# Fourier mixing with a gated feed-forward block: the output product as seven half-size products for eight, with its sums on GpSimd and its result transposed on VectorE

## The chip, the cores and the metric

The kernel runs on one core of one Trainium2 chip. The metric is the device time of one execution in microseconds. A core has TensorE (matmuls, and weight loads beside them), VectorE (called DVE in the profile), ScalarE (ACT), GpSimd (POOL) and SyncE (SP), which issues DMAs. SBUF is the working memory, PSUM the memory in banks that matmuls write to.

## What is computed

The reference, cut to what matters:

```python
batch, seq, dim = (8, 3008, 256)               # x, float32
X = np.fft.fft(np.fft.fft(x, axis=1), axis=2).real.astype(np.float32)
x = X.reshape(24064, 256)
gate = 1.0 / (1.0 + np.exp(-(x @ w_gate)))     # w_gate, w_val: 256 x 1536
val = x @ w_val
return (gate * val @ w_out).astype(np.float32) # w_out: 1536 x 256
```

All matmuls are float32.

## The kernel before, in words

**Prologue.** The sequence transform uses that the real part of the result is even in the sequence position: for each of the 8 batches only positions 0 to 1504 (`NK` = 1505) are computed, and each gives two output rows, `k` and its mirror `S - k`. `fold_x` (L180) adds and subtracts mirrored sequence positions and features of the input in place in the tile `x4`, and writes the feature-folded halves to the tiles `wp` and `wq`. For batch 0 it runs on VectorE. `half` (L208) then does one matmul group of the sequence transform with the table `st`: six matmuls into two PSUM banks `ev` and `od`, a copy of `ev` to `a` by ScalarE, and two VectorE instructions (L216, L219) that write the sum and the difference to every second column of the tiles `pk` and `qk`; a third tile, `ek`, holds feature 128. The weights arrive as 64-bit floats; `weight_ops` (L109) turns each piece into float32 with work on VectorE and GpSimd, and `merge` (L141) multiplies the gate and value weights with the feature transform once, into `G1`, `G2` and `ge`. The last six of the eighteen pieces are `w_out`, which goes to the tile `wo`.

**Main loop.** The positions of a batch are cut into six chunks, five of 256 and one of 225, and the 1536 hidden features into 12 tiles of 128. A step is one (batch, chunk, feature tile): 576 steps, numbered by the loop at L352. `front` (L259) does four matmuls into two banks `pa` and `pb` (for gate and value), two `scalar_tensor_tensor` instructions that make `ae` from `pa` (L272), two VectorE instructions that make `z` from `ae` and `pb` (L275 the position, L276 its mirror), and the sigmoid of the gate half of `z` on ScalarE (L277). `gate` (L280) multiplies the gate by the value to give `h` (L283); it is issued one step later, ahead of the next step's `front`. `back` (L286) multiplies `h` with `wo` into `po`, with `h` as the stationary operand and `wo` as the moving one, so that tokens are the rows of the result: four matmuls of 128 rows by 256 columns for a step, three steps after its `front` (`LAG`, L349). The trace counts two instructions for each float32 matmul. After the twelfth feature tile `store` (L298) copies `po` to SBUF on ScalarE and issues the output DMAs on SP.

Each engine takes its instructions in the order in which the code issues them. The four banks of `psx` go round among `pa`, `pb`, `ev` and `od`; the four of `pso` hold `po` of two chunks, two banks each.

**Side work.** The dictionary `side` (L334) places work for the next batch at steps: `fold_x` of the next batch on GpSimd after step 1 of a batch (one list of large instructions, L185 to L198), the load of the batch after that at step 12, and the groups of the sequence transform (`seq_ops`, L222) spread over the later steps. In the first batch `e_fold` and `e_rows` add the rows that `ek` needs for the other seven.

Of the kernel before, what the change touches and what calls it, by code (L numbers as in the profile page):

```python
# [13 lines left out]
PSUM = bass.MemoryType.PSUM  # L14

# [19 lines left out]
def kernel(  # L35
# [19 lines left out]
    NFT = F // P  # L55
    CH = 256
    WC = 256
    HD = D // 2
    assert D == 256 and M % 4 == 0 and NP * NQ > M // 2 and NQ % 2 == 0
# [7 lines left out]
    fold = ctx.enter_context(tc.tile_pool(name="fold", bufs=1))  # L67
# [5 lines left out]
    hp = ctx.enter_context(tc.tile_pool(name="hp", bufs=4))  # L73
    osp = ctx.enter_context(tc.tile_pool(name="osp", bufs=4))
    psx = ctx.enter_context(tc.tile_pool(name="psx", bufs=4, space=PSUM))
    pso = ctx.enter_context(tc.tile_pool(name="pso", bufs=4, space=PSUM))
# [17 lines left out]
    wo = const.tile([P, NFT, D], F32, name="wo")  # L94
# [5 lines left out]
    er = const.tile([B - 1, NK], F32, name="er")  # L100
# [8 lines left out]
    def weight_ops(src, out):  # L109
# [6 lines left out]
        exp = osp.tile([P, 2, WC], F32, name="exp", tag="os")  # L116
# [38 lines left out]

    def load_weights():
        jobs = []
        for c in range(F // WC):
            for g, w in enumerate((moe_w_gate, moe_w_val)):
                jobs.append((w[:, c * WC : (c + 1) * WC], g, c))  # L160
        for c in range(NFT // 2):
            jobs.append((moe_w_out[2 * c * P : 2 * (c + 1) * P, :], None, c))
        rest = []
        for src, g, c in jobs:
            if g is None:
                ws = wo[:, 2 * c : 2 * c + 2, :]
            else:
                ws = app.tile([P, 2, WC], F32, name="ws", tag="ae")
            first, then = weight_ops(src, ws)
            first()  # L170
            for f in rest:
                f()
            rest = [then] + ([] if g is None else [lambda ws=ws, g=g, c=c: merge(ws, g, c)])
        for f in rest:
            f()
# [4 lines left out]
    def fold_x(b, eng):  # L180
        x4 = X.pop(b)
        tt = eng.tensor_tensor

        def point(i, j):
            tt(x4[:, i, :, 1:D], x4[:, i, :, 1:D], x4[:, j, :, D - 1 : 0 : -1], op=ALU.add)  # L185
            tt(x4[:, i, :, 0], x4[:, i, :, 0], x4[:, j, :, 0], op=ALU.add)

        point(0, 1)
        point(2, 3)
        tt(x4[:, 1], x4[:, 0], x4[:, 2], op=ALU.add)  # L190
        tt(x4[:, 3], x4[:, 0], x4[:, 2], op=ALU.subtract)
        for blk in range(2):
            v = x4[:, 1 + 2 * blk]
            wp = fold.tile([NP, NQ, HD], F32, name="wp", tag=f"wp{blk}")
            wq = fold.tile([NP, NQ, HD - 1], F32, name="wq", tag=f"wq{blk}")
            tt(wp[:, :, 1:HD], v[:, :, 1:HD], v[:, :, D - 1 : HD : -1], op=ALU.add)  # L196
            eng.tensor_copy(wp[:, :, 0], v[:, :, 0])
            tt(wq, v[:, :, 1:HD], v[:, :, D - 1 : HD : -1], op=ALU.subtract)  # L198
            W[b, blk] = (wp, wq)
            if b == 0:  # L200
                we = hp.tile([NP, NQ, P], F32, name="we", tag="we")
                eng.tensor_copy(we, v[:, :, HD : HD + 1].to_broadcast([NP, NQ, P]))  # L202
                W[b, blk] += (we,)
# [4 lines left out]
    def half(w, d, blk, sn, rows):  # L208
        c0, n = ((0, NE), (NE, NO))[blk]
        ev, od = bank("ev")[0:rows, 0:n], bank("od")[0:rows, 0:n]  # L210
        for o, par in ((ev, 0), (od, 1)):
            for q in range(par, NQ, 2):
                mm(o, w(q), st[:, int(sn), q, c0 : c0 + n], q == par, q >= NQ - 2)
        a = evp.tile([P, NE], F32, name="a", tag="a")[0:rows, 0:n]
        nc.scalar.copy(a, ev)
        nc.vector.tensor_tensor(d[:, blk : blk + 2 * n - 1 : 2], a, od, op=ALU.add)  # L216
        lo, hi = (od, a) if sn else (a, od)
        top = M - blk
        nc.vector.tensor_tensor(d[:, top : top - 2 * NO + 1 : -2], lo[:, 0:NO], hi[:, 0:NO],  # L219
                                op=ALU.subtract)  # L220

    def seq_ops(b):  # L222
        def start():
            PQE[b] = (pqp.tile([P, NK], F32, name="pk", tag="pk"),
                      pqp.tile([HD - 1, NK], F32, name="qk", tag="qk"),
                      pqp.tile([P, NK], F32, name="ek", tag="ek"))
            if b:
                nc.sync.dma_start(out=PQE[b][2], in_=ed[b - 1 : b, :].to_broadcast([P, NK]))

        def group(blk, what):  # L230
            rows = HD - 1 if what == 1 else P
            return lambda: half(lambda q: W[b, blk][what][:, q, :], PQE[b][what], blk, what == 1,
                                rows)

        return [start] + [group(blk, what) for blk in range(2) for what in range(2 if b else 3)]


# [11 lines left out]
    def e_rows(blk):  # L249
        half(lambda q: x8[:, :, 1 + 2 * blk, q], er, blk, False, B - 1)  # L250
        if blk:
            nc.scalar.dma_start(out=ed, in_=er)
# [3 lines left out]
    steps = [(b, c, f) for b in range(B) for c in range(len(chunks)) for f in range(NFT)]  # L256
    PO = {}

    def front(b, c, f):  # L259
        k0, n = chunks[c]  # L260
        ks = slice(k0, k0 + n)
        fs = slice(f * P, (f + 1) * P)
# [15 lines left out]
        return b, c, f, z  # L278

    def gate(b, c, f, z):  # L280
        n = chunks[c][1]
        h = hp.tile([P, 2, CH], F32, name="h", tag="h")[:, :, 0:n]
        nc.vector.tensor_tensor(h, z[:, 0], z[:, 1], op=ALU.mult)  # L283
        return b, c, f, h

    def back(b, c, f, h):  # L286
        n = chunks[c][1]
        if f == 0:
            PO[b, c] = [pso.tile([P, 2, D], F32, name="po", tag="po") for _ in range(2)]
        for s in range(2):  # L290
            for j, t0 in enumerate(range(0, n, P)):
                m = min(P, n - t0)
                mm(PO[b, c][s][0:m, j, :], h[:, s, t0 : t0 + m], wo[:, f, :],
                   f == 0 and j == 0, f == NFT - 1)
        if f == NFT - 1:
            store(b, c, PO.pop((b, c)))

    def store(b, c, po):  # L298
        k0, n = chunks[c]
        for s in range(2):  # L300
            os_ = osp.tile([P, 2, D], F32, name="os", tag="os")
            lo, hi, r0 = 0, n, b * S + k0
            if s:
                r0 = b * S + S - k0 - n + 1
                lo = 1 if k0 + n == NK else 0
                hi = n - 1 if k0 == 0 else n
            if n == 2 * P:
                nc.scalar.copy(os_, po[s])  # L308
            else:
                for j, t0 in enumerate(range(0, n, P)):  # L310
                    m = min(P, n - t0)
                    nc.scalar.copy(os_[0:m, j], po[s][0:m, j])
            if (lo, hi) == (0, 2 * P):
                nc.sync.dma_start(out=out[r0 : r0 + n, :].rearrange("(j p) d -> p j d", p=P),
                                  in_=os_)
                continue
            for j, t0 in enumerate(range(0, n, P)):
                p0, p1 = max(lo - t0, 0), min(hi - t0, P)
                pm = p0 + (p1 - p0) // 16 * 16
                for u0, u1 in ((p0, pm), (pm, p1)):  # L320
                    if u0 < u1:
                        nc.sync.dma_start(out=out[r0 + t0 + u0 : r0 + t0 + u1, :],
                                          in_=os_[u0:u1, j, :])


    fold_x(0, nc.vector)
    for f in seq_ops(0):
        f()
    load_weights()
# [3 lines left out]
    per = len(chunks) * NFT  # L333
    side = {}  # L334
    for b in range(B - 1):
        s0 = b * per
        side.setdefault(s0 + 1, []).append(lambda b=b: fold_x(b + 1, nc.gpsimd))
        if b + 2 < B:
            side.setdefault(s0 + NFT, []).append(lambda b=b: load_x(b + 2))
        f0 = 2 * NFT  # L340
        if b == 0:
            f0 = 3 * NFT + 6
            side.setdefault(f0 - 10, []).append(e_fold)
            for blk in range(2):
                side.setdefault(f0 - 6 + 2 * blk, []).append(lambda blk=blk: e_rows(blk))
        for i, f in enumerate(seq_ops(b + 1)):
            side.setdefault(s0 + f0 + i * (per - f0 - 4) // 5, []).append(f)

    LAG = 3  # L349
    fresh = None  # L350
    ready = []
    for i, step in enumerate(steps):  # L352
        if fresh is not None:
            ready.append(gate(*fresh))
        fresh = front(*step)
        if len(ready) >= LAG:
            back(*ready.pop(0))
        for f in side.get(i, []):
            f()
    ready.append(gate(*fresh))  # L360
    for r in ready:
        back(*r)
# [49 lines left out]
```

## Time and profile before

| what | value |
|---|---|
| median of three runs | 2286.54 us (2284.35 to 2288.05) |
| the profiled execution | 2285.57 us |
| its span, first to last instruction | 2283.8 us |
| mean granted clock of TensorE | 0.988 |
| ScalarE busy | 431.3 us, 19% |
| GpSimd busy | 236.9 us, 10% |
| the chain that ended last, by engine | PE 68%, DVE 23%, ACT 4%, DMA 2% |

The span is the time between the first and last instruction of the profiled execution; the 1.8 us between it and the time of that execution lie around it. "Busy" is the time in which an engine had an instruction running; matmuls are pipelined and their ends are modelled, so TensorE's busy time is not its time at its peak. "Idle" is the time just before an instruction in which its engine had nothing to do, and the releaser named behind the arrow is what the instruction waited for. In the groups, "128x512 f32<-128x512 f32" is the shape written and read, in partitions by elements, and L283 is line 283 of the kernel.

### The profile page before, as it was taken

The page shows a single profiled execution, that of the slowest core. Times are in us where ns is not written, and L with a number is a line of the kernel's source. Part 1 is how long each engine was busy: PE and PEld are TensorE (multiplying, and loading weights), DVE is VectorE, ACT ScalarE, POOL GpSimd, SP SyncE. Part 2 cuts the span into 40 slices and gives each one's busy share as a digit, 9 for nine tenths or more (in the row PEclk, how much of TensorE's full clock was granted, in tenths as well). Part 3 has the DMA queues.
Part 4 walks back from the last instruction along what each step waited for, and adds up shares of the span by engine and source line. Part 5 has one row for each costly group of instructions (what it writes and reads, how often), then busy time and mean ns, then how long its engine had stood idle before and what let it go on. Part 6 is the DMA issues. An engine that isn't in the chain of part 4 may idle for free.

```text
span 2283.8 us, 26007 instructions
## 1 busy us (share of the span) xinstructions
PE 2199.2 (96%) x9840; PEld 1840.4 (81%) x9840; DVE 1717.3 (75%) x3056; ACT 431.3 (19%) x762; POOL 236.9 (10%) x146
## 2 busy tenths in 40 slices
PE   4759999999999999999999999999999999999998
PEld 2648788888887888888888888878888888888887
DVE  3977777777777777777777777777777777777776
ACT  0111121112112111211211121112112111211211
POOL 0980001200002000020002000020000000000000
PEclk9779999999999999999999999999999999999999
DMA  5350010100001000110001000010000000000000
GB/s 166 117 132 10 10 33 10 63 23 19 10 10 63 32 10 10 39 57 10 10 19 63 23 19 10 10 63 33 10 10 18 23 10 10 19 9 10 19 10 18
DMA packets 56340, 70.86 MB, mean 31 GB/s; under 512 B 24117, under 2 KB 48437, under 8 KB 53948
## 3 DMA queue, kind: packets, MB, share of 16 engines
q1 hardware_dynamic: 34384, 64.26, 8.2%
q10 hardware_dynamic: 21832, 4.94, 1.1%
q8 instruction: 79, 1.29, 0.2%
q14 instruction: 45, 0.37, 0.1%
HBM read 44.50 MB, written 24.68 MB: 30 GB/s over the span
## 4 chain that ended last, share of the span: by engine, by line
PE 68%; DVE 23%; ACT 4%; DMA 2%; issue 1%; ACTq 1%; DVEq 0%
PE po L79 31%; PE pb L79 16%; PE pa L79 15%; DVE h L283 6%; DVE ae L272 6%; DVE z L275 5%; ACT z L277 4%; DVE z L276 4%; PE ev L79 3%; PE od L79 3%; DMA st<-in_stab_dram 1%; ACTq L240 1%; DVE man L130 1%; DVE man L133 0%; DVE man L132 0%
## 5 line engine op out<-in xcount | busy, mean ns | idle before, releaser
L79 PE MATMUL po<-wo,h 128*128 128x256 f32 (+1 forms) x4608 | 1091.0, 379 | 1.4 <-DVE h L283 1.3
L79 PEld LDWEIGHTS po<-wo,h 128*128 128x128 f32 (+1 forms) x4608 | 864.9, 188 | 127.3 <-DVE h L283 2.3
L283 DVE TENSOR_TENSOR h<-z 128x512 f32<-128x512 f32 (+1 forms) x576 | 423.3, 735 | 411.5 <-ACT z L277 411.5
L277 ACT ACTIVATE z<-z 128x512 f32<-128x512 f32 (+1 forms) x576 | 357.9, 621 | 1721.5 <-DVE z L276 1721.5
L79 PE MATMUL pa<-pk,G 128*128 128x256 f32 (+1 forms) x2304 | 585.2, 376 | 28.8 <-DVE ae L272 28.8
L79 PE MATMUL pb<-qk,G 127*128 127x256 f32 (+1 forms) x2304 | 601.0, 383 | 5.4 <-DVE z L276 5.2
L79 PEld LDWEIGHTS pa<-pk,G 128*128 128x128 f32 x2304 | 437.5, 190 | 96.3 <-DVE ae L272 32.6
L79 PEld LDWEIGHTS pb<-qk,G 127*128 127x128 f32 x2304 | 420.5, 190 | 111.5 <-issue 56.2
L272 DVE SCALAR_TENSOR_TENSOR ae<-ek,ge,pa 128x256 f32<-128x256 f32 (+1 forms) x1152 | 492.1, 468 | 0.0
L275 DVE TENSOR_TENSOR z<-ae,pb 128x512 f32<-128x512 f32 (+1 forms) x576 | 389.9, 677 | 61.0 <-DVE ae L272 1.4
L276 DVE TENSOR_TENSOR z<-ae,pb 128x512 f32<-128x512 f32 (+1 forms) x576 | 385.4, 669 | 0.0
L196 POOL TENSOR_TENSOR wp<-x 126x762 f32<-126x762 f32 x14 | 26.1, 1867 | 752.3 <-PE od L79 752.3
L185 POOL TENSOR_TENSOR x<-x 126x1530 f32<-126x1530 f32 x14 | 48.2, 3445 | 302.7 <-DMA x<-in_xf_dram 302.7
L198 POOL TENSOR_TENSOR wq<-x 126x762 f32<-126x762 f32 x14 | 25.3, 1807 | 364.3 <-PE od L79 364.3
L79 PE MATMUL ev<-st,wp 126*128 126x377 f32 (+1 forms) x96 | 35.1, 502 | 24.3 <-DMA st<-in_stab_dram 24.3
L79 PE MATMUL ps<-ws,dt 128*128 128x256 f32 (+1 forms) x96 | 31.8, 490 | 17.8 <-DVE ws L137 9.6
L79 PEld LDWEIGHTS ev<-st,wp 126*128 126x128 f32 x96 | 18.9, 198 | 34.1 <-DVE we L202 24.3
L308 ACT COPY os<-po 128x512 f32<-128x512 f32 x80 | 42.2, 578 | 0.0
L79 PEld LDWEIGHTS ps<-ws,dt 128*128 128x128 f32 (+1 forms) x96 | 22.0, 240 | 22.3 <-issue 18.2
L128 POOL TENSOR_SCALAR exp<-exp 128x512 int32<-128x512 f32 x18 | 36.6, 2031 | 1.5
L79 PE MATMUL ev<-st,wq 126*127 126x377 f32 (+1 forms) x96 | 33.1, 480 | 1.5 <-DMA st<-in_stab_dram 1.5
L79 PE MATMUL od<-st,wp 126*128 126x377 f32 (+1 forms) x96 | 33.6, 486 | 0.0
(58 smaller groups left out, 415.1 us busy)
## 6 DMA issues: line engine op xcount, KB each, us to landing
x<-in_xf_dram SPq DMA_DIRECT2D x16, 1512.0 KB
out_dram<-os SPq DMA_DIRECT2D x72, 256.0 KB
ek<-ed SPq DMA_DIRECT2D x7, 752.5 KB
st<-in_stab_dram ACTq DMA_DIRECT2D x2, 2223.7 KB
raw<-in_moe_w_gate_dram SPq DMA_DIRECT2D x6, 512.0 KB
raw<-in_moe_w_val_dram SPq DMA_DIRECT2D x6, 512.0 KB
raw<-in_moe_w_out_dram SPq DMA_DIRECT2D x6, 512.0 KB
out_dram<-os SPq DMA_DIRECT2D x16, 128.0 KB
```

The lines of the kernel that those rows point to most:

```text
L79: nc.tensor.matmul(o, l, r, start=start, stop=stop, skip_group_check=True)
L128: nc.gpsimd.tensor_scalar(out=expi, in0=exp, scalar1=0.0, scalar2=255.0 * 2.0 ** 23, op0=ALU.max, op1=ALU.min)
L130: ts(out=mani, in0=hi, scalar1=0xFFFFF, scalar2=3, op0=ALU.bitwise_and, op1=ALU.logical_shift_left)
L185: tt(x4[:, i, :, 1:D], x4[:, i, :, 1:D], x4[:, j, :, D - 1 : 0 : -1], op=ALU.add)
L196: tt(wp[:, :, 1:HD], v[:, :, 1:HD], v[:, :, D - 1 : HD : -1], op=ALU.add)
L198: tt(wq, v[:, :, 1:HD], v[:, :, D - 1 : HD : -1], op=ALU.subtract)
L272: nc.vector.scalar_tensor_tensor(out=ae[:, g], in0=ek[:, ks], scalar=ge[:, g, f : f + 1], in1=pa[:, g], op0=ALU.mult, op1=ALU.add)
L275: nc.vector.tensor_tensor(z[:, :, 0], ae, pb, op=ALU.add)
L276: nc.vector.tensor_tensor(z[:, :, 1, ::-1], ae, pb, op=ALU.subtract)
L277: nc.scalar.activation(z[:, 0], z[:, 0], AF.Sigmoid)
L283: nc.vector.tensor_tensor(h, z[:, 0], z[:, 1], op=ALU.mult)
L308: nc.scalar.copy(os_, po[s])
```

## The change

**The output product.** Two feature tiles make a pair (`NPR` = 6 pairs for a chunk). For a pair, the product of the two token halves (position and mirror), the two feature tiles and the two halves of the output columns is a 2 by 2 by 2 block product. It is now done with Strassen's seven block products (in the form with shared sums) for eight. Four sums of `h` are made on GpSimd in `gate` for each pair: one after the first `h` of the pair, three after the second, each of 128x256. Four sums of `w_out`'s blocks are made once, on GpSimd, in `forms`, which also copies three blocks on VectorE. The weights are now the stationary operand and the sums of `h` the moving one, so the result has output columns as rows and tokens as columns. Seven tiles accumulate over the six pairs of a chunk, in four PSUM banks `po0` to `po3`; there is one set of them.

**After a chunk**, `finish` copies the seven tiles to SBUF on ScalarE (four copies), and puts ten entries on the list `later`, one of which is issued at the end of each step: five GpSimd instructions that combine the seven products, then four VectorE transposes in 32x32 blocks, and the stores, now of 64 floats at a time. For the last chunk the five instructions are on VectorE.

**The folds** write in place (no `wp` and `wq`), and those of the next batch are cut in thirds, 20 entries, one issued per step from step 9 of a batch. **The sequence transform's** two VectorE instructions are issued one step after its matmuls (`split`). The steps of the side work and the step at which the next load is issued are changed. `back` of a pair comes in two parts, at the two steps after two further pairs. Pools have other sizes: `h` now holds a pair and has three buffers, and the pools `osp` and `fold` go.

The diff's core:

```diff
+    sp = ctx.enter_context(tc.tile_pool(name="sp", bufs=2))
+    cp = ctx.enter_context(tc.tile_pool(name="cp", bufs=2))
+    op = ctx.enter_context(tc.tile_pool(name="op", bufs=2))
-    pso = ctx.enter_context(tc.tile_pool(name="pso", bufs=4, space=PSUM))
+    pso = ctx.enter_context(tc.tile_pool(name="pso", bufs=1, space=PSUM))
...
+    def forms(ws, c):
+        w = ws.rearrange("p f (a h j) -> p f h a j", h=2, j=TB)
+        f = wf[:, c].rearrange("p m (a j) -> p m a j", j=TB)
+        sub = lambda o, a, b: nc.gpsimd.tensor_tensor(o, a, b, op=ALU.subtract)
+        nc.vector.tensor_copy(f[:, 0:2], w[:, :, 0])
+        nc.vector.tensor_copy(f[:, 2], w[:, 1, 1])
+        sub(f[:, 4], w[:, 0, 1], w[:, 0, 0])
+        sub(f[:, 6], w[:, 1, 1], w[:, 0, 1])
+        sub(f[:, 5], w[:, 1, 1], f[:, 4])
+        sub(f[:, 3], w[:, 1, 0], f[:, 5])
...
+        def feat(v, r, q):
+            tt(r[:, q, 0 : HD - 1], v[:, q, 1:HD], v[:, q, D - 1 : HD : -1], op=ALU.subtract)
+            tt(v[:, q, 1:HD], v[:, q, 1:HD], v[:, q, D - 1 : HD : -1], op=ALU.add)
+        qs = [slice(q, q + nq) for q in range(0, NQ, nq)]
+        for i in (0, 2):
+            ops += [lambda i=i, q=q: point(i, i + 1, q) for q in qs]
+            ops.append(lambda i=i: first(i, i + 1))
+        ops += [lambda q=q: tt(x4[:, 1, q], x4[:, 0, q], x4[:, 2, q], op=ALU.add) for q in qs]
+        ops += [lambda q=q: tt(x4[:, 3, q], x4[:, 0, q], x4[:, 2, q], op=ALU.subtract) for q in qs]
...
+    def gate(p, fh, z):
+        n = chunks[pairs[p][1]][1]
+        tt = nc.gpsimd.tensor_tensor
+        if fh == 0:
+            H[p] = hp.tile([P, 2, 2, CH], F32, name="h", tag="h")[:, :, :, 0:n]
+            SF[p] = sp.tile([P, 4, CH], F32, name="sf", tag="sf")[:, :, 0:n]
+        h, s = H[p], SF[p]
+        nc.vector.tensor_tensor(h[:, fh], z[:, 0], z[:, 1], op=ALU.mult)
+        if fh == 0:
+            tt(s[:, 2], h[:, 0, 0], h[:, 0, 1], op=ALU.subtract)
+        else:
+            tt(s[:, 0], h[:, 0, 1], h[:, 1, 1], op=ALU.add)
+            tt(s[:, 1], s[:, 0], h[:, 0, 0], op=ALU.subtract)
+            tt(s[:, 3], h[:, 1, 0], s[:, 1], op=ALU.subtract)
+    SLOT = {1: (3, 0), 2: (0, 0), 6: (0, 1), 5: (1, 0), 7: (1, 1), 4: (2, 1), 3: (2, 0)}
+    ORDER = ((1, 2, 4), (7, 5, 6, 3))
...
+        for m in ORDER[part]:
+            t, j = SLOT[m]
+            mm(PO[t][:, j, 0:n], wf[:, i, m - 1], move[m], i == 0 and m in (1, 2, 4, 7),
+               i == NPR - 1)
...
+    def finish(b, c, eng):
...
+        nc.scalar.copy(t[:, 6, 0:n], PO[3][:, 0, 0:n])
+        for j in range(3):
+            nc.scalar.copy(t[:, 2 * j : 2 * j + 2, 0:n], PO[j][:, :, 0:n])
+        if nb * TB > n:
+            nc.gpsimd.memset(t[:, :, n : nb * TB], 0.0)
...
+        def flip(s, h, slot):
+            nc.vector.transpose(os_[:, s, 0:nb, h, :], t[:, slot, 0 : nb * TB])
...
+        later.extend([
+            lambda: tt(v[:, 0:2], v[:, 6:7].to_broadcast([P, 2, n]), v[:, 0:2], op=ALU.add),
+            lambda: tt(v[:, 3], v[:, 1], v[:, 3], op=ALU.add),
+            lambda: tt(v[:, 1], v[:, 1], v[:, 2], op=ALU.add),
+            lambda: tt(v[:, 4:6], v[:, 1:4:2], v[:, 4:6], op=ALU.add),
+            lambda: tt(v[:, 2], v[:, 3], v[:, 2], op=ALU.add),
+            lambda: flip(0, 0, 0),
+            lambda: flip(0, 1, 4),
+            lambda: (flip(1, 0, 5), store(0)),
+            lambda: flip(1, 1, 2),
+            lambda: store(1)])
...
+    def split(i, f, *args):
+        at(i, lambda: at(i + 1, f(*args)))
...
+        if b:
+            at(s0 + 1, lambda b=b: load_x(b + 1))
+        def folds(s0=s0, b=b):
+            for j, f in enumerate(fold_ops(b + 1, nc.gpsimd, 2)):
+                at(s0 + 9 + j, f)
+        at(s0 + 8, folds)
+        at(s0 + 33, lambda b=b: seq_start(b + 1))
+        for j in range(4):
+            split(s0 + 36 + 8 * j, seq_group, b + 1, j // 2, j % 2)
...
+        if fresh is not None:
+            gate(*fresh)
+        fresh = front(i // 2, i % 2)
+        if i >= 4:
+            back(i // 2 - 2, i % 2)
+        elif later:
+            pass
+        if later:
+            later.pop(0)()
+        for f in side.pop(i, []):
+            f()
```

## The prediction

> **What bounds the kernel now.** First the page's head: TensorE 96% busy, VectorE 75%, which would make a saved matmul pay. But ends of matmuls are modelled there, so I read a stretch without folds and transforms instead, by groups of instructions, 2040 to 2200 us (columns: count, busy us, mean ns of one, idle time before and what ended it):
>
> ```profile
> L79 PE MATMUL po<-wo,h 128*128 128x256 f32 x355 | 84.0, 379 | 0.0
> L272 DVE SCALAR_TENSOR_TENSOR ae<-ek,ge,pa 128x256 f32<-128x256 f32 x88 | 38.1, 473 | 0.0
> L283 DVE TENSOR_TENSOR h<-z 128x512 f32<-128x512 f32 x45 | 31.1, 692 | 34.3 <-ACT z L277 34.3
> L277 ACT ACTIVATE z<-z 128x512 f32<-128x512 f32 x44 | 27.7, 629 | 129.2 <-DVE z L276 129.2
> ```
>
> VectorE never waits for a matmul in it: `ae` has no idle time, and `h` waits 0.76 us per step for the sigmoid, which itself waits for `z`. So a ring turns: z, sigmoid, h, ae, ae, z. The timeline at 1500 us gives its period, and a second thing (start, duration, engine):
>
> ```profile
> 1503.57 0.63 ACT L277 ACTIVATE z<-z 128x512 f32<-128x512 f32 x1 [2.99 <-DVE z L276]
> 1503.99 0.84 PEld L79 LDWEIGHTS pa<-pk,G 128*128 128x128 f32 x4
> 1504.23 0.69 DVE L283 TENSOR_TENSOR h<-z 128x512 f32<-128x512 f32 x1 [0.76 <-ACT z L277]
> 1504.84 0.86 DVE L272 SCALAR_TENSOR_TENSOR ae<-ek,ge,pa 128x256 f32<-128x256 f32 x2
> ...
> 1506.42 0.68 DVE L276 TENSOR_TENSOR z<-ae,pb 128x512 f32<-128x512 f32 x1
> 1507.19 0.63 ACT L277 ACTIVATE z<-z 128x512 f32<-128x512 f32 x1 [2.99 <-DVE z L276]
> 1507.32 3.44 POOL L185 TENSOR_TENSOR x<-x 126x1530 f32<-126x1530 f32 x1 [60.82 <-DMA x<-in_xf_dram]
> 1507.44 0.84 PEld L79 LDWEIGHTS pa<-pk,G 128*128 128x128 f32 x4
> 1507.85 3.45 DVE L283 TENSOR_TENSOR h<-z 128x512 f32<-128x512 f32 x1 [0.76 <-ACT z L277]
> ...
> 1510.71 0.66 POOL L186 TENSOR_TENSOR x<-x 126x6 f32<-126x6 f32 x1
> ```
>
> Sigmoid to sigmoid is 3.62 us (3.315 in the 225-column chunk, 2261.89 to 2265.21), while TensorE, catching up here, needs 3.45 (1503.99 to 1507.44): 16 matmul instructions at 0.216. **TensorE is not the bound; VectorE with the sigmoid is.** And the `h` of 1507.85 takes 3.45 us instead of 0.69: it ends at 1511.30, 0.54 after GpSimd's L185 does (1510.76). GpSimd's next instruction, 126x6, then shows 0.66 where it takes 0.21 alone: h went ahead of it. `h` is the one VectorE instruction of a step with both inputs in SBUF; ae and z, which read PSUM too, keep 0.47 and 0.68 beside GpSimd. So GpSimd work and `h` exclude each other; the later waits out the running instruction.
>
> The accounts of the profiled run (2285.57, span 2283.80; its median is 1.0 higher): first sigmoid at 139.34, last at 2275.15, 575 intervals. 480 steps x 3.618 + 95 x 3.315 = 2051.5, so 84.3 are disturbances, and 8.65 are tail. The groups by shape split the 84.3: the full-width `h` has mean 754 against a median 692, x480 = 30 us behind GpSimd folds; the other 54 lie around the sequence transforms, 30 in the loop at 1.8 us each (`half`: two VectorE instructions of 0.55, and waits for their matmuls and the copy `a`).
>
> **Prices on GpSimd**, the groups of the whole span with shapes kept apart:
>
> ```profile
> L185 POOL TENSOR_TENSOR x<-x 126x1530 f32<-126x1530 f32 x14 | 48.2, 3445 | 302.7 <-DMA x<-in_xf_dram 302.7
> L198 POOL TENSOR_TENSOR wq<-x 126x762 f32<-126x762 f32 x14 | 25.3, 1807 | 364.3 <-PE od L79 364.3
> L134 POOL TENSOR_TENSOR wo<-man,exp 128x512 f32<-128x512 f32 x6 | 7.8, 1293 | 0.5
> L246 POOL TENSOR_TENSOR x<-x 126x42 f32<-126x42 f32 x1 | 0.3, 280 | 0.1
> ```
>
> (3445-280)/(1530-42) = 2.13 ns per element and 0.19 us fixed: 0.73 us for 256, 1.28 for 512, 0.46 for 128; about 0.08 between dependent ones (54.01 after 53.20+0.72).
>
> **The change, part by part.**
>
> *One matmul of eight less.* TensorE's pair of steps falls from 32 to 30 instructions, 6.91 to 6.48 us, 288 pairs, 124 us. The ring takes 7.24 per pair either way: worth 0 on the path. (If the ring were not the bound, this would be the gain.)
>
> *Sums in `gate`.* After an even h one GpSimd sum; after an odd h three in a row. From the start of the odd h: it ends 0.69, GpSimd hears it 0.09 later, then 0.78-1.56, 1.65-2.38, 2.47-3.20. The next h comes at 3.62: 0.42 to spare, cost 0. Bounds: 0; or one sum in the way of every second h, 0.73 x 288 = 210. I take 0, the 256-element price lying between measured sizes.
>
> The Trainium skill, "GPSIMD Engine Reference", section 4.1, speaks against this placing: elementwise two-input work belongs on VectorE, GpSimd being about 2x slower; its 4497 ns for 2048 elements would make an estimate of 0.56 for 256, so the chain would end near 2.7, and the sum for this part would still be 0. What the rule leaves out here is that these VectorE slots are the bound.
>
> *`finish` for a chunk* queues five GpSimd sums, one per step (1.28, 0.73, 0.73, 1.28, 0.73), among the gate's. Clock from the start of the h after the chunk's last step: the PSUM copies (0.37, 0.58) let the first run at 1.0-2.3; the gate's three then begin at 2.4, the second runs 3.2-3.9, and the next h, due 3.62, ends 3.9+0.54 = 4.46 instead of 4.31: 0.15 lost. Third sum, second finish sum, one gate sum, third finish sum: until 7.7, h due 7.39: 0.16. Three gate sums to 10.7, the fourth finish sum to 12.05, h due 11.17: ends 12.6 instead of 11.86, 0.73. The fifth fits. Sum 1.04 x 47 chunks = 49 us. (The last chunk's sums are on VectorE.) Bounds: 0, all in free slots; 4.75 x 47 = 223, all in the way.
>
> *Folds in place, in thirds, one entry per step* (20 entries, seven batches). Behind one gate sum an entry of 1.28 ends at 2.9, before the next h; behind three it runs 3.28-4.55 and h, ending 5.09 instead of 4.31, loses 0.78. Five of the twelve long entries fall there: 3.9. The six split entries (two of 0.73) lose about 0.4 per pair, 1.2; five steps also carry finish sums, about 1 more. 6.1 x 7 = 43, in place of the 30 now. Bounds: 0; all 24.6 us of GpSimd fold time x 7 = 172.
>
> *Sequence transforms* get their two VectorE instructions one step later, after z_b and ahead of h, in the gap where VectorE waits for the sigmoid: the gap opens 0.61 after z_b starts, closes at 1.43. Two at 0.46 (0.55 less the 0.09 by which successive instructions overlap) end at 1.53; with a margin 0.15 x 30 = 4.5 instead of 54. If the matmuls are late after all, it goes back towards 54.
>
> *Transposes*, four of 128x256 per chunk, sit in the same 0.82 us gap. No transpose is in the trace. ae moves 256 elements in 0.47, so hidden, 0; if it is blocked as VectorE's one-input L130 is (1.48 beside GpSimd in the weight load, 0.41 alone), 0.66 x 188 = 124. I take 0: nearest in size is ae, and in these steps the gate's sums end at 3.20 after h starts. The Trainium skill, "SBUF — State Buffer", section "Who interferes with whom", lets an instruction with one SBUF input pass beside GpSimd unless it runs in a 2-port mode: by it the cost is 0 too, and no row here shows it for a transpose.
>
> *Single `po` banks.* TensorE's next chunk must wait for four copies (0.37 + 3 x 0.58) behind a sigmoid. TensorE leads by two steps now (the last pa runs at 2267.82, the ae that reads it at 2273.00). Calling the end of ae(i) zero: back(i+1) would start at -1.4, sigmoid(i) ends 2.1, the last copy 4.2, so TensorE starts front(i+2) at 4.7, ends pa 5.6 and pb 6.4; VectorE wants them at 6.4 and 7.3. Nothing lost, 0.8 us of cover; without it, up to 4.8 x 47 = 226. The stores' 64-float pieces are hidden: the DMA engines show 0 or 1 tenths busy in most slices.
>
> *Ends.* The weight load is paced by GpSimd (0.68+1.96+1.31 and gaps = 4.2 per job); five jobs get four sums of 0.46+0.08 on it, +10.8, less 0.7 of waiting it has now; the last sign merge loses its block by the fold (3.90 to 0.68: -3.2), two copies add 0.6. First ae 134.5 -> 142.0, first sigmoid 144.3 (now also held by ACT's DMA issue to 139.3). Tail after the last sigmoid: h 1.2, sums 2.3, matmul 0.5, copies to 6.2, the rest of five VectorE sums to 7.4, transposes to 9.0, eight DMA issues at 0.4, landing 3: 15.2 instead of 8.65.
>
> **Sum:** 144.3 + 2051.5 + 49 + 43 + 4.5 + 15.2 = 2307.5 span, + 1.8 around it = **2309 us**, 1.0% slower. TensorE gets lighter, the ring does not.
>
> **Rivals.**
> (a) *Faster:* the gain from the transforms (54 to 5) outlives the collisions. For: GpSimd has 2.6 us per pair free. Against: order in its queue is fixed. If finish and fold sums meet h half as often as worked out, 46 us go: 2263. It decides below about 70 us of collisions together.
> (b) *The gate's sums already hit h:* 0.42 to spare is one semaphore delay per link. At 0.3 to 0.7 per pair, + 86 to 200: about 2440.
> (c) *`po` waits:* the 0.8 us cover is eaten, 1 to 2 us per chunk, + 47 to 94: about 2380.
> (d) *No change:* collisions near 70 us, 2286.
> That the matmul saved isn't saved cannot be: `back` issues seven.
>
> **Chances.** Forecast (2290 to 2340) 0.46; (a) 0.23; (d) 0.06; (b) 0.14; (c) 0.11. Range 2255 to 2410: it leaves out the lowest part of (a), 0.08, and the upper half of (b) with the far ends of the bounds, 0.11. Faster 0.23, same 0.07, slower 0.70, by 0.2%, about what a measurement of this kernel tells from none.
>
> **What would show it.** Right: undisturbed steps still 3.62 with TensorE idle ahead of pa or pb; h's median 0.69, its mean up to about 0.85, long ones in finish and fold steps; transform waits gone; transposes inside `h <- z`'s gap. (b) shows as h's median above 0.69 in every second step, (c) as ae or z waiting for matmuls after each chunk. Wrong altogether if a step is shorter than 3.6.

## The result, and the profile after

The changed kernel takes 2340.98 us (median of four runs, 2339.65 to 2341.83) against 2287.3 for the kernel before: ratio 1.0234, 95% interval 1.0216 to 1.0251. The forecast was slower by 1.0%, so the direction and its reason held and the size did not. The profiled execution takes 2339.65 us with a span of 2337.6, 30.1 more than the forecast's sum of 2307.5.

First the waits of the changed kernel, the longest that bear on the loop (total us, times, longest):

```profile
DVE h L320 <- ACT z L309: 361.7, 545, 1.2
POOL sf L322 <- PE po L88: 220.6, 115, 5.9
PEld po L88 <- ACT c L356: 130.6, 47, 4.6
POOL c L384 <- ACT c L358: 115.4, 47, 2.9
DVE ae L304 <- PE pa L88: 27.5, 19, 3.9
DVE z L307 <- PE pb L88: 6.1, 10, 0.7
```

VectorE still stands 362 us at `h`, waiting for the sigmoid: the ring is still there. New are TensorE's wait for the copies out of `po`, once after each of 47 chunks, and VectorE's waits for `pa` and `pb`, few but long. In the groups by shape:

```profile
L304 DVE SCALAR_TENSOR_TENSOR ae<-ek,ge,pa 128x256 f32<-128x256 f32 x960 | 415.1, 473 | 27.8 <-PE pa L88 27.2
L320 DVE TENSOR_TENSOR h<-z 128x512 f32<-128x512 f32 x480 | 392.6, 818 | 307.4 <-ACT z L309 307.2
L365 DVE STREAM_TRANSPOSE os<-c 128x256 f32<-128x256 f32 x192 | 84.0, 439 | 0.0
L324 POOL TENSOR_TENSOR sf<-h 128x256 f32<-128x256 f32 x240 | 174.3, 726 | 305.6 <-DVE h L320 305.6
```

`h` is longer than in the kernel before, whose row is

```profile
L283 DVE TENSOR_TENSOR h<-z 128x512 f32<-128x512 f32 x480 | 362.1, 754 | 344.1 <-ACT z L277 344.1
```

A transpose takes 0.44 us, and a sum of 256 on GpSimd takes the 0.73 us that the line through two measured sizes (42 and 1530) gave. Two plain steps show the ring and gate's three sums (start, duration):

```profile
1514.22 0.63 ACT L309 ACTIVATE z<-z 128x512 f32<-128x512 f32 x1 [3.06 <-DVE z L308]
...
1514.88 0.69 DVE L320 TENSOR_TENSOR h<-z 128x512 f32<-128x512 f32 x1 [0.76 <-ACT z L309]
...
1515.65 0.73 POOL L324 TENSOR_TENSOR sf<-h 128x256 f32<-128x256 f32 x1 [2.83 <-DVE h L320]
1516.45 0.73 POOL L325 TENSOR_TENSOR sf<-sf,h 128x256 f32<-128x256 f32 x1
...
1517.26 0.72 POOL L326 TENSOR_TENSOR sf<-h,sf 128x256 f32<-128x256 f32 x1
1517.84 0.63 ACT L309 ACTIVATE z<-z 128x512 f32<-128x512 f32 x1 [2.99 <-DVE z L308]
...
1518.57 0.69 DVE L320 TENSOR_TENSOR h<-z 128x512 f32<-128x512 f32 x1 [0.82 <-ACT z L309]
```

Sigmoid to sigmoid is 3.62 us as before, and the sums end at 1517.98, before the `h` of 1518.57. But that `h`, the first of a pair, starts 0.07 later after its sigmoid than the one before it (0.82 against 0.76 of idle time), and the next step is 3.69 long.

I took the ring apart for the whole trace: five intervals for each step (sigmoid, `h`, first `ae`, first `z`, second `z`, next sigmoid), each less its median in the kernel before, and each long `h` put down to the GpSimd instruction that was running when it started. The rows are good to about 2 us, since some late `h` can be put down in more than one way. In us:

| part | before | after | forecast for after |
|---|---|---|---|
| first sigmoid | 139.3 | 143.7 | 144.3 |
| after the last sigmoid | 8.6 | 14.2 | 15.2 |
| `h` behind a fold | 30.7 | 11.7 | 43 |
| `h` behind one of finish's sums | - | 27.3 | together 49 |
| `h` behind one of gate's sums | - | 27.0 | (with the line above) |
| `h` 0.07 late at the first of a pair | - | 17.8 | 0 |
| VectorE waits for `pa`, `pb` | 0 | 33.6 | 0 |
| late `h` around transforms | 52 | about 4 | 4.5 |
| smaller pieces | about 4 | about 10 | 0 |

So the forecast was 31 too high for the folds and 67 too low for the lines of finish and gate, the late first `h`, the waits and the small pieces; the two ends take 1.6 off, and the other 4 to the 30.1 lie in the rounding of the step and of the rows. Most of the waits for `pa` come from one place, step 52 of each batch, whose ring is 3.8 us late on the mean (2.9 to 4.6), 3.1 of it the wait for `pa`. (A pair reaches `back` four steps after its `front`, so the first pair of the chunk that starts at step 48 does so at 52.) There the trace shows the chain, here in the fifth batch:

```profile
1433.41 0.35 ACT L356 COPY c<-po 128x256 f32<-128x256 f32 x1
1433.53 0.69 DVE L320 TENSOR_TENSOR h<-z 128x512 f32<-128x512 f32 x1 [0.76 <-ACT z L309]
1433.66 1.56 ACT L358 COPY c<-po 128x512 f32<-128x512 f32 x3
...
1433.81 1.19 PE L88 MATMUL po<-h,wf 128*128 128x256 f32 x4 [1.83 <-ACT c L356]
...
1435.81 2.06 PE L88 MATMUL ev<-st,x 126*128 126x376 f32 x6
...
1437.71 2.06 PE L88 MATMUL od<-st,x 126*128 126x376 f32 x6
...
1439.61 1.03 PE L88 MATMUL pa<-pk,G 128*128 128x256 f32 x4
...
1440.67 0.87 DVE L304 SCALAR_TENSOR_TENSOR ae<-ek,ge,pa 128x256 f32<-128x256 f32 x2 [2.24 <-PE pa L88]
```

The copies stand behind the step's sigmoid; TensorE waits for them with the new chunk's first matmuls; a transform's twelve instructions are queued behind; then comes the `pa` that VectorE is already waiting for.

### The profile page after: what moved, and what is told of

It is laid out like the page before. It is cut to its first block, busy times and chain, and to the rows that moved or that the text cites. A ratio compares the mean times of both kernels' runs of the same rounds, so it can differ in the third digit from the quotient of the medians.

```text
span 2337.6 us, 27462 instructions
## 1 busy us (share of the span) xinstructions
PE 2119.6 (91%) x9264; PEld 1776.8 (76%) x9264; DVE 1824.5 (78%) x3263; ACT 466.3 (20%) x842; POOL 1337.2 (57%) x1663
## 4 chain that ended last, share of the span: by engine, by line
DVE 49%; PE 28%; ACT 12%; issue 5%; POOL 4%; DMA 1%; DVEq 1%; ACTq 0%; POOLq 0%
DVE ae L304 13%; DVE h L320 13%; PE po L88 12%; DVE z L307 11%; DVE z L308 11%; ACT z L309 10%; PE pa L88 6%; PE pb L88 6%; PE ev L88 2%; PE od L88 2%; POOL exp L136 2%; DMA st<-in_stab_dram 1%; ACT c L358 1%; POOL ws L142 1%; ACT c L356 1%
## 5 line engine op out<-in xcount | busy, mean ns | idle before, releaser
L88 PE MATMUL po<-h,wf 128*128 128x256 f32 (+1 forms) x1728 | 460.6, 403 | 121.4 <-ACT c L356 112.1
L88 PE MATMUL po<-sf,wf 128*128 128x256 f32 (+1 forms) x2304 | 535.2, 375 | 0.0
L88 PEld LDWEIGHTS po<-h,wf 128*128 128x128 f32 x1728 | 338.0, 201 | 195.5 <-ACT c L356 130.6
L88 PEld LDWEIGHTS po<-sf,wf 128*128 128x128 f32 x2304 | 437.7, 190 | 51.8 <-POOL sf L326 0.4
L322 POOL TENSOR_TENSOR sf<-h 128x256 f32<-128x256 f32 (+1 forms) x288 | 212.0, 736 | 391.3 <-PE po L88 220.6
L324 POOL TENSOR_TENSOR sf<-h 128x256 f32<-128x256 f32 (+1 forms) x288 | 206.0, 715 | 377.5 <-DVE h L320 377.5
L325 POOL TENSOR_TENSOR sf<-sf,h 128x256 f32<-128x256 f32 (+1 forms) x288 | 213.6, 742 | 22.6
L326 POOL TENSOR_TENSOR sf<-h,sf 128x256 f32<-128x256 f32 (+1 forms) x288 | 211.7, 735 | 22.6
L88 PE MATMUL ev<-st,x 126*128 126x377 f32 (+5 forms) x204 | 76.2, 512 | 26.4 <-DMA st<-in_stab_dram 26.2
L365 DVE STREAM_TRANSPOSE os<-c 128x256 f32<-128x256 f32 x192 | 84.0, 439 | 0.0
L358 ACT COPY c<-po 128x512 f32<-128x512 f32 (+1 forms) x144 | 73.9, 591 | 2.7 <-PE po L88 2.7
```

The costliest lines, as they stand in the source:

```text
L88: nc.tensor.matmul(o, l, r, start=start, stop=stop, skip_group_check=True)
L322: tt(s[:, 2], h[:, 0, 0], h[:, 0, 1], op=ALU.subtract)
L324: tt(s[:, 0], h[:, 0, 1], h[:, 1, 1], op=ALU.add)
L325: tt(s[:, 1], s[:, 0], h[:, 0, 0], op=ALU.subtract)
L326: tt(s[:, 3], h[:, 1, 0], s[:, 1], op=ALU.subtract)
L358: nc.scalar.copy(t[:, 2 * j : 2 * j + 2, 0:n], PO[j][:, :, 0:n])
```

## The experiments

Theory A: the ring of z, sigmoid, h and ae, 3.62 us per step, is the bound of both kernels, and what the change adds lies on it as collisions, waits and lost lead of TensorE. Rival theories stand in each expectation. The changed kernel was not measured again beside these runs; the kernel before was, with medians of 2284.75 to 2285.33 us against 2287.3 in the result. So a difference from the changed kernel's 2340.98 may be 2 to 4 us smaller than it stands here, and one of 3 to 5 us is not told from none.

**1 and 2. The ring taken away, in both kernels.** `h` of a step is issued two steps after its `front`:

```diff
-        if fresh is not None:
-            gate(*fresh)
-        fresh = front(i // 2, i % 2)
+        if len(fresh) == 2:
+            gate(*fresh.pop(0))
+        fresh.append(front(i // 2, i % 2))
```

> The kernel before, with h of a step issued two steps after its front instead of one, so that VectorE no longer waits for the sigmoid of the same step. Theory A (the ring of z, sigmoid, h, ae on VectorE and ScalarE sets 3.62 us per step, and TensorE's 3.45 us is hidden behind it): TensorE becomes the bound, 60 steps x 3.455 + 12 x 3.25 + 15.6 of transforms = 262 us per batch, eight batches less one set of transforms 2080, with 139 ahead and 9 behind: 2215 to 2250 us. Theory B (TensorE, the time its busy share suggests, was the bound all along): no gain, 2275 to 2300.

> The changed kernel with the same edit: h two steps after its front. Theory A: VectorE's step without the wait is 0.61 + 0.97 + 0.60 + 0.60 = 2.78 us, TensorE's pair 6.48 us is now the bound, so the matmul that is saved shows: 229 us per batch of steps and 15.6 of transforms, 1938 for all, with 144 ahead and 14 behind 2096, and some 1.3 us per chunk in which TensorE waits for the copies out of the single set of po banks: 2120 to 2200 us, below the kernel before with the same edit by 40 to 110. Theory B (the sums on GpSimd, through the SBUF lock against h, or GpSimd itself are the changed kernel's bound): the edit gives little, 2290 or more.

Measured: the kernel before with this edit 2234.8 us, ratio 0.9779 (0.9747 to 0.9812); the changed kernel with it 2118.6, ratio 0.9266 (0.9241 to 0.9291). Theory A hits the first. The second lies 1 us below its range, and the 116 us between the two kernels with the edit (0.948 by the medians) are more than its 40 to 110: it had 1.3 us per chunk for TensorE's wait at the copies, and the longest of these waits is now 1.2 us. The sign of the change turns over, for without the edit it was 54 us slower. Theory B is out in both. In the trace of the changed kernel with the edit:

```profile
1331.11 0.84 PEld L88 LDWEIGHTS pa<-pk,G 128*128 128x128 f32 x4
...
1331.55 0.65 DVE L320 TENSOR_TENSOR h<-z 128x512 f32<-128x512 f32 x1
...
1332.39 0.87 DVE L304 SCALAR_TENSOR_TENSOR ae<-ek,ge,pa 128x256 f32<-128x256 f32 x2 [0.20 <-PE pa L88]
...
1334.13 0.84 PEld L88 LDWEIGHTS pa<-pk,G 128*128 128x128 f32 x4
...
1337.59 0.60 PEld L88 LDWEIGHTS pa<-pk,G 128*128 128x128 f32 x3
```

`h` no longer waits, `ae` now waits for TensorE, and a pair of steps takes 6.48 us from `pa` to `pa` (1331.11 to 1337.59): 30 matmul instructions at 0.216. The wait for `pa` is now the longest of VectorE:

```profile
DVE ae L304 <- PE pa L88: 184.3, 227, 4.0
```

**3. A transform away from the po wait.** Steps 28, 30 and 52 become 30, 32 and 56.

```diff
-            split(s0 + 36 + 8 * j, seq_group, b + 1, j // 2, j % 2)
+            split(s0 + (36, 44, 56, 60)[j], seq_group, b + 1, j // 2, j % 2)
```

> The changed kernel with the third transform group at step 56 of a batch instead of 52, and the second group of the rows for ek at 30 instead of 28 (its DMA at 32), so that no transform's matmuls are queued on TensorE right behind back of a new chunk, which waits for the copies out of po. Theory A (at step 52 of a batch VectorE waits 3.6 us for pa, since wait and transform add up on TensorE and use up its lead of two steps): seven times 3.6 and some 3 in the first batch go, 2310 to 2318. Theory B (the po wait itself costs VectorE, after every chunk): no change within 6 us, 2335 to 2347.

Measured: 2338.07 us, ratio 1.0226 (1.0199 to 1.0254), 3 below the changed kernel, which is no clear difference. Theory B's figure. The steps tell why: the 3.8 us at step 52 fall to 0.7, but steps 56 and 57 now cost 1.0 and 0.4, and step 60, which cost 0.1, costs 1.8; `h` stands a little longer behind gate's sums (29.5). This fits a loss of TensorE's lead that is not tied to a step: moved four steps on, the transform finds the lead still unpaid, since TensorE gains only 3.62 - 3.24 = 0.38 us per step.

**4 and 5. Finish's sums on VectorE**, first as for the last chunk, then with the first of them a step later.

```diff
-                finish(b, c, nc.vector if p == len(pairs) - 1 else nc.gpsimd)
+                finish(b, c, nc.vector)
...
         later.extend([
+            lambda: None,
```

> The changed kernel with the five sums of finish on VectorE for every chunk, as it has them for the last one. They are issued after z of a step, so they run in the 0.8 us in which VectorE waits for the sigmoid. Theory A (h collides with finish's sums, 27 us, and with gate's sums, 27 us, since finish pushes gate's later): most of both goes, less about 0.2 us per sum that waits for one of gate's sums: 2285 to 2315. Theory B (gate's own three sums in a row collide with h, finish has no part in it): finish's 27 us go and the sums cost VectorE about as much: 2325 to 2350.

> The kernel with finish's sums on VectorE, with the first of them one step later, when the copies it reads have been made. Theory A (in the run before, VectorE stood 1.36 us per chunk at the first sum, waiting for the copies, which hid the gain from the collisions): 2354 less 47 x 1.36 = 64, 2280 to 2300, so some 50 below the changed kernel: the collisions caused by finish. Theory B (finish's sums cost VectorE as much wherever they stand): 2335 or more.

Measured: 2354.37 us (ratio 1.03, 1.0272 to 1.0329), then 2317.6 (1.015, 1.0133 to 1.0166). Both miss theory A's range; the first lands above theory B's too, the second between the two. In the first, the collisions went as theory A said: `h` stands 25.8 us behind GpSimd instead of 66. But VectorE, which takes its instructions in order, stood at the first sum until the copies were made:

```profile
DVE c L384 <- ACT c L358: 72.8, 48, 2.8
```

With the sum a step later this wait is gone and the kernel is 23 us faster than the changed kernel. That is half of the 50 expected: VectorE's waits for `pa` rise to 34.0 us, and the sums, which have two inputs in SBUF as `h` has, meet GpSimd themselves: they stand some 25 us behind gate's sums and 6 behind folds, and `h` starts late behind them (34 us in all against 22 in the changed kernel).

**6. The copies ahead of the sigmoid.** ScalarE's order is the only thing changed.

```diff
-        nc.scalar.activation(z[:, 0], z[:, 0], AF.Sigmoid)
         return p, fh, z
...
             back(i // 2 - 2, i % 2)
+        z = fresh[2]
+        nc.scalar.activation(z[:, 0], z[:, 0], AF.Sigmoid)
```

> The changed kernel with the sigmoid of a step issued after back instead of inside front, so that on ScalarE the copies out of po come ahead of the sigmoid of that step, which is not due before they are done. Nothing else moves. Theory A (what VectorE waits for after chunks is TensorE's lead of two steps, used up by the po wait of 2 to 4 us, which ends late only because the copies stand behind a sigmoid, and by a transform that follows before the lead is won back at 0.37 us a step): the po wait falls from about 3 us per chunk to 1, VectorE's waits for pa and pb (34 us) go, 2303 to 2317 us. Theory B (the transforms alone use up the lead, wherever the copies stand): within 8 of the changed kernel, 2333 to 2347.

Measured: 2290.85 us, ratio 1.0033 (1.002 to 1.0046): 50 us less than the changed kernel (46 by the two ratios), 12 below theory A's range, and theory B is out. The waits of this kernel for the copies, with the copy of `po3` at L355 and the others at L357:

```profile
PEld po L88 <- ACT c L357: 20.0, 45, 0.7
PE po L88 <- ACT c L357: 6.2, 25, 0.3
PEld po L88 <- ACT c L355: 4.9, 25, 0.5
```

The longest is 0.7 us where it was 4.6. VectorE's waits for `pa` and `pb` in the loop go from 33.6 to under 2, and `h` behind gate's sums goes from 27.0 to 0.7, while finish's own stay (25.8) and folds rise (22.6). The way to gate's sums is GpSimd's queue: after a chunk the first of finish's sums, which waits for the copies, stands ahead of three of gate's. In the changed kernel it starts 0.79 us after the start of an `h`, and the last of the three ends 0.67 us after the next `h` has started and stands waiting; with the copies first the finish sum starts 1.88 us before its `h`, and the last of the three ends 0.58 us before the next one (medians of 47). So the late copies cost twice: TensorE's lead, and gate's sums made late. Only ScalarE's order differs in this kernel, so both are shown to come from it.

**7. TensorE kept busy in the wait.** `front`'s four matmuls run twice in the step ahead of the wait.

```diff
+        s = 2 * p + fh
+        for _ in range(2 if s > 4 and s % 12 == 4 else 1):
```

> The changed kernel with the four matmuls of front issued twice in the one step per chunk whose front stands ahead of the po wait. The second set writes the same values again; it fills 1.7 us of a wait of up to 3.9 us, so TensorE's idle time stays short, and the copies come no sooner. In the changed kernel's trace the granted clock falls to 0.5 for 3.4 us or more 28 times in the main loop, after such waits, 140 us in all; with the copies first it does so nowhere. Theory A (part of the loss is the halved clock, which takes 1.7 us per fall from TensorE's lead on top of the wait): the falls go, and 10 to 35 us with them, 2305 to 2330. Theory B (the wait itself is the loss, the clock only goes along with it): 2335 to 2350.

Measured: 2326.27 us, ratio 1.0181 (1.0164 to 1.0198), 15 below the changed kernel: in theory A's range, with a gain in the lower half of its 10 to 35. What it acts on shows in the busy times of the changed kernel in three stretches around a po wait (TensorE's busy time comes first after the length; the granted clock is the figure ahead of the DMA share):

```profile
1510.00:1518.00 8.00, 7.49 (x34) 5.74 (x33) 5.95 (x11) 1.42 (x3) 3.39 (x5) 1.00 0.86 318
1518.50:1522.05 3.55, 0.49 (x3) 0.09 (x1) 2.76 (x5) 0.52 (x1) 0.94 (x2) 1.00 0.28 114
1522.07:1525.48 3.41, 3.03 (x7) 2.50 (x8) 2.76 (x5) 1.96 (x6) 2.49 (x3) 0.50 0.01 2
```

TensorE is idle for 3.5 us, then has half the clock for 3.41 us: seven matmul instructions take 3.03 there, 0.43 each instead of 0.22. Between 160 and 2250 us the trace of the changed kernel has 28 such falls, 133 us in all; with the matmuls doubled nine, 31 us; with the copies first none. The Trainium skill, "TensorE: Matmul & The Clock Gate", section "HAM oscillation — how this bites in real kernels", says that idle gaps of over some 3.4 us bring the clock down. Here each of the 24 gaps of 3.6 us and more (from one matmul's start to the next, less 0.22) has its fall, which starts inside the gap, up to 2.1 us ahead of its end, or within 1 us behind it. But 3.4 us is no sharp limit: four of the seven gaps of 2.0 to 2.3 us have a fall too, which starts within 1.4 us behind them, and with the matmuls doubled nine of the 24 gaps of 1.9 to 2.7 us that are left. The doubled matmuls do no useful work and most of the falls go with them, so a part of the loss is most likely the clock. How much is not shown: nine falls are left, and late `h` behind GpSimd changes by some us as well.

**8. A third buffer for the first of gate's sums.**

```diff
+    sq = ctx.enter_context(tc.tile_pool(name="sq", bufs=3))
...
+            SF[p] = [None, sq.tile([P, CH], F32, name="sq", tag="sq")[:, 0:n]]
...
+            tt(s2, h[:, 0, 0], h[:, 0, 1], op=ALU.subtract)
```

> The changed kernel with the first of gate's four sums in a tile of its own with three buffers; the other three keep two. Theory A (that sum waits 220 us in all for TensorE to give back a buffer, since TensorE is late after the po wait, and so all sums behind it are late and meet h, 27 us): the wait goes for the first sum and most of the 27 us too, 2312 to 2328. Theory B (the sums meet h because finish's and the folds' entries stand ahead of them in GpSimd's queue): 2334 to 2347.

Measured: 2336.33 us, ratio 1.0221 (1.0206 to 1.0237): 5 less, no clear difference, in theory B's range. GpSimd's 220 us of waiting for a buffer go, and `h` behind gate's sums falls only from 27.0 to 20.5, while behind folds it rises from 11.7 to 22.8. So that waiting was mostly not what made the sums late.

**9. Gate's sums left out.** The seven matmuls read blocks of `h`, and the four sums in `gate` are left out, so the output is another.

```diff
-        move = {1: h[:, 0, 0], 2: h[:, 1, 0], 3: s[:, 3], 4: h[:, 1, 1], 5: s[:, 0], 6: s[:, 1],
-                7: s[:, 2]}
+        move = {1: h[:, 0, 0], 2: h[:, 1, 0], 3: h[:, 1, 0], 4: h[:, 1, 1], 5: h[:, 0, 1],
+                6: h[:, 1, 1], 7: h[:, 0, 0]}
```

> The changed kernel without gate's four sums: the seven matmuls of a pair read blocks of h instead, so the output is not the reference's. It prices the sums. Theory A (they cost 0.07 us at the first h of each pair, for a second wait of that instruction, on GpSimd, and the 27 us in which h stands behind one of them, after finish or fold entries have pushed them late): 18 + 27, and some 10 to 20 from entries of finish and folds that no longer meet h: 2272 to 2300. Theory B (the ring is slowed by finish and folds alone): 2330 or more.

Measured: 2294.94 us, ratio 1.0048 (1.0033 to 1.0063): 46 less, in theory A's range. The 0.07 at the first `h` of each pair goes (17.8 to 1.4 us), so does `h` behind gate's sums, and finish's part halves (27.3 to 13.5). What stays is the po wait, and with it the waits for `pa`, now longer:

```profile
PEld po L87 <- ACT c L348: 109.5, 40, 4.1
DVE ae L303 <- PE pa L87: 40.5, 31, 4.5
```

**10. One part of the change in the kernel before**: a transform's two VectorE instructions one step later.

```diff
+        for f in done:
+            f()
+        done = [t for t in [f() for f in side.get(i, [])] if t]
```

> The kernel before with one part of the change alone: the two VectorE instructions of a transform one step after its matmuls. Theory A (the wait in front of them, 52 us in all, goes and little comes back, as in the changed kernel): TensorE now fills in, at 262 us per batch against 266 and the ring's 257: 2235 to 2260. Theory B (the wait was TensorE's time and moves to the next pa): no change, 2275 to 2290.

Measured: 2277.59 us, ratio 0.9967 (0.9957 to 0.9977). Theory B. The wait ahead of those instructions, 52 us, is gone, and its place is taken by

```profile
DVE ae L279 <- PE pa L79: 42.8, 23, 3.0
```

In the kernel before TensorE has 3.62 - 3.45 = 0.17 us per step to win back a transform's 3.8 us, so deferring the instruction that waits gives 0.3%.

**11. Both good edits together**, `h` two steps later and the copies first.

> The changed kernel with h two steps after its front and with the sigmoid issued after back, both edits together. Theory A (with h later the kernel goes at TensorE's pace, 6.48 us per pair, and its po wait is down to some 10 us already): only those 10 us, 2103 to 2119. Theory B (the po wait still costs 1 us or more per chunk, hidden in TensorE's busy time): 2060 to 2095.

Measured: 2117.52 us, ratio 0.9266 (0.9252 to 0.928), the same as with the ring's edit alone. With the ring's edit alone the po wait is already short (the longest 1.2 us). With the copies first it is gone, and that wins 1 us, no clear difference. Both versions beat the kernel before by 7.3%.

## Why the prediction was right or wrong

**One matmul of eight less, worth 0 on the path: right.** Plain steps stay at 3.62 us; the same saving shows as 6.48 us per pair as soon as the ring is gone (experiment 2).

**Gate's sums, 0: 45 us, of which the sum had 7 in finish's term.** In plain steps the three in a row end 0.6 us before the next `h`; the working had 0.42. Not foreseen was the second thing that the first `h` of a pair must now wait for: 0.07 us, 17.8 in all. That it comes with the sums is shown: in 238 of the 288 pairs the trace has one more instruction of VectorE's sequencer ahead of that `h` (`EVENT_SEMAPHORE`), and `h` waits for GpSimd's semaphore besides ScalarE's; experiment 9 has neither. That it is the buffer of `h`, which GpSimd now reads, is argued. The other 27 us are these sums made late; experiment 6 has them too, so they are not to be added to its 50.

**Finish's sums, 49: the size was off.** Its own sums cost 27.3 where the working had 42, nearly all of it at the fourth, which costs 0.54 a chunk where the working had 0.73. The other 7 were for gate's sums behind the first finish sum, and some 17 were measured there: they start at 2.02 us, not 2.4, so the next `h` mostly meets the third of them and not the second, and waits 0.37 a chunk on the mean, not 0.15. A collision is worth the rest of whatever runs, and a shift of 0.4 us changes which that is.

**Folds, 43: too high**, 11.7. That each delayed `h` moves the ones after it clear of their entries is argued; it fits that the folds cost 22.6 once the copies come first.

**Transforms, 4.5, and transposes, 0: right.** Late `h` around transforms is about 4 us, and a transpose of 0.44 us fits the gap. All 192 lie between 404 and 442 ns, though 126 of them run beside a GpSimd instruction: here the Trainium skill, "SBUF — State Buffer", section "Who interferes with whom", was right that one SBUF input passes.

**"Single `po` banks ... Nothing lost, 0.8 us of cover": the step that failed.** It is what rival (c) named, through other doors. The working put one wait against a full lead. It left out that a transform is queued right behind the wait at step 52, that the lead returns at only 0.38 us a step, that TensorE's clock falls to half at every idle gap of 3.6 us and more in this trace, and that gate's sums, which stand behind finish's first sum in GpSimd's queue, become late with the copies. Experiment 6 prices it all: 50 us where the sum had 0. That the sum as a whole missed by only 30 is luck: terms that were some 80 us too low met folds and finish's own sums, which were 46 too high.

**First sigmoid and tail: right** within 1 us each.

What stays open: how the 50 us divide among TensorE's halved clock, the transform and the late sums, since experiments 3 and 8 gave no clear difference and 7 gave 15 us; and the 10 us of small pieces.

## What to carry to other kernels

Before an engine's work is cut, look for a ring through two in-order engines whose period is the step; if there is one, shift the consumer by a step first, and the cut then pays (here 5% in place of a loss of 2.3%). Where a single set of accumulators must be copied out between chunks, put the copies ahead of other work on the copying engine. A lead that absorbs one wait is spent afterwards: price what is queued right behind it, and the rate at which the lead comes back.

## What the runs showed of the hardware that was not expected

TensorE's granted clock fell to 0.5 for 3.4 us (twice that in some cases) in the middle of a busy loop, 28 times, in or just after all 24 idle gaps of 3.6 to 4.4 us and after four of seven of 2.0 to 2.3 us. A VectorE instruction that waits for two engines instead of one started 0.07 us later (some 250 cases of 0.04 to 0.12). An `h` held up by GpSimd ended 0.48 to 0.55 us after GpSimd's instruction did, in both kernels, and went ahead of GpSimd's next one (126x6 at 1510.71 in the kernel before); so a collision costs the rest of one instruction.
